# Masks, transposes and turned sums of a causal attention put into other TensorE tilings, with filler matmuls at the start

## The chip, the core and the metric

The kernel runs on one core of a Trainium2 chip. The metric is the device time of one execution in microseconds; the time of a kernel is the median of its runs. Engines are called PE (TensorE; its weight loads are PEld), DVE (VectorE), ACT (ScalarE), POOL (GpSimd) and SP (SyncE, which issues every DMA).

## The reference

```python
scores = q @ k.T / 8                      # 2 x 12 heads, 448 queries, 64 wide
scores = where(causal mask, -1e9, scores)
p = exp(scores - rowmax);  p /= (p.sum(-1) + 1e-9)
x = (p @ v) as 896 tokens x 768
h = x @ w_in                              # 768 -> 2048
g = max(h, 0) + alpha * min(h, 0)
x2 = g @ w_out                            # 2048 -> 768
g2 = sigmoid(x2 @ w_gate) * (x2 @ w_val)  # 768 -> 1536, twice
out = g2 @ w_out2                         # 1536 -> 768
```

All inputs of the attention are fp32; the weights arrive as fp64 words and are turned into fp32 on the core.

## The kernel before, in words

**Attention.** The 24 heads go in 12 pairs m. The two heads of a pair lie in partitions 0-63 and 64-127 of one tile `raw` (q and k, queries in columns). Queries and keys are cut into four chunks of 112. For each pair, `scores` (L445) computes in three groups, chunk 3, then chunks 2 and 0, then chunk 1. A score matmul has 64 rows, so that the two heads' matmuls lie in two row tiles of the array; fp32 needs two passes, each its own record. Ahead of each group `mask` (L434) writes the causal mask of the diagonal block with an identity of 112 rows in bf16, one matmul for each head.

DVE takes the negative row maxima (L464), ACT the exponentials with their sums (L475). `transposes` (L507) turns p in ten 112x112 blocks for each head into the PSUM tiles `t` (112 rows, the whole array); `copy_p` (L519) copies them to `pt` in three copies of 448, 448 and 224 columns, shared by ACT and DVE. `values` (L531) multiplies by v with 112 rows and 64 columns: the two heads lie in two column tiles. In between, `inverses` (L481) inverts the sums (112x8), `turn_sums` (L487) transposes them on PE, `copy_sums` (L492) copies them out, `spill` (L496) and `spread` (L500) take them through DRAM and spread each over 64 partitions (`rb`), and `scale_x` (L542) multiplies the result in `pv` by `rb`. POOL splits it into two fp32r parts, `xh` (L553) and `xl` (L558).

So PE works in three tilings: the whole array (masks, transposes, turned sums and all products of the feed-forward layers), two row tiles (scores), two column tiles (values).

**Feed-forward layers.** Every product is three fp32r matmuls of 128x128 by 448 columns (L631 to L633). A block of weights is loaded as words (`load_w`, L575), and turned into fp32 and split by ACT and DVE (`w_abs` L585, `w_clamp` L590, `w_shift` L595, `w_sign` L600, `w_low` L607, `w_hi` L620, `w_lo` L624). For the first four blocks `w_clamp` and `w_lo` run on POOL. The first three blocks (`NFILL`, 36 products, 108 matmuls) are "fill": they may run between the heads; those of the first six pairs' tokens need pair 5 split, those of the others pair 11.

**Order.** A planner (`Plan`, L88) writes the instruction order of all engines ahead of time: a list schedule over tasks with costs in ns, ring buffers (`take`, `use`), and a rank `base + OFFSET` that decides among tasks which could start at the same time. A task that changes PE's tiling (`mode`) is charged 185 ns. Tasks marked `late` follow only when all others are placed. PSUM has eight banks: `s0`, `s1`, `t`, `pv`, two of each. Every engine then executes in program order and waits on semaphores.

**Start.** 16 bf16 matmuls of 224 columns (L755) run ahead of the first scores. SP's first loads are, in order, q and k of pair 0, alpha, v of pair 0, weights 0, pair 1, weights 1, pair 2, weights 2.

Of the kernel before, what the change touches and what calls it, by code (L numbers as in the profile page):

```python
# [38 lines left out]
V_ORDER = (0, 3, 1, 2)
# [6 lines left out]
    ("load",): -58.635, ("load_v",): 7.783, ("scale_q",): -14.461, ("mask", 0): -68.882, ("scores", 0): -13.369,  # L46
    ("mask", 1): 11.629, ("scores", 1): -41.229, ("mask", 2): -10.666, ("scores", 2): 3.508, ("maxima", 3): -33.522,
    ("expo", 3): 77.499, ("maxima", 2): -23.050, ("expo", 2): -6.102, ("maxima", 0): -19.609, ("expo", 0): -68.639,
    ("maxima", 1): -5.168, ("expo", 1): -39.932, ("transposes", 0): -3.281, ("copy_p", 0): 49.609,
    ("transposes", 1): 2.477, ("copy_p", 1): -39.851, ("transposes", 2): -56.207, ("copy_p", 2): -58.597,  # L50
    ("values", 0): 6.339, ("values", 3): -46.358, ("values", 1): -75.999, ("values", 2): 7.714,
    ("inverses",): -60.677, ("turn_sums",): -8.582, ("copy_sums",): -11.583, ("spill",): 40.514, ("spread",): 71.632,
    ("scale_x",): -0.940, ("split_x",): -51.504, ("split_x_lo",): -23.205, None: -17.857, ("load_w", 0): 9.850,
    ("w_abs", 0): 50.945, ("w_clamp", 0): -37.063, ("w_shift", 0): -29.708, ("w_sign", 0): -30.857,
    ("w_low", 0): 6.510, ("w_hi", 0): -4.303, ("w_lo", 0): -3.032, ("h", 0, 0): 12.860, ("neg", 0, 0): 47.449,
    ("pos", 0, 0): 68.908, ("add", 0, 0): -83.306, ("g_hi", 0, 0): -8.976, ("g_lo", 0, 0): -51.651,
    ("h", 0, 1): -18.475, ("neg", 0, 1): 36.331, ("pos", 0, 1): -59.901, ("add", 0, 1): 74.082,
    ("g_hi", 0, 1): 12.898, ("g_lo", 0, 1): 6.457, ("load_w", 1): -155.678, ("w_abs", 1): 57.861,
    ("w_clamp", 1): -6.859, ("w_shift", 1): -0.546, ("w_sign", 1): -19.022, ("w_low", 1): 9.102, ("w_hi", 1): 34.782,
    ("w_lo", 1): -69.814, ("h", 1, 0): 47.300, ("neg", 1, 0): 2.091, ("pos", 1, 0): -4.691, ("add", 1, 0): 21.461,  # L60
    ("g_hi", 1, 0): -1.670, ("g_lo", 1, 0): -70.870, ("h", 1, 1): -3.830, ("neg", 1, 1): 18.865,
    ("pos", 1, 1): 41.081, ("add", 1, 1): 13.413, ("g_hi", 1, 1): 36.660, ("g_lo", 1, 1): -40.749,
    ("load_w", 2): 36.339, ("w_abs", 2): 34.065, ("w_clamp", 2): 23.745, ("w_shift", 2): -21.161,
    ("w_sign", 2): 50.694, ("w_low", 2): -5.847, ("w_hi", 2): 9.976, ("w_lo", 2): -1.386, ("h", 2, 0): 14.568,
    ("neg", 2, 0): -9.107, ("pos", 2, 0): -20.582, ("add", 2, 0): -33.620, ("g_hi", 2, 0): -17.520,
    ("g_lo", 2, 0): 14.456, ("h", 2, 1): 9.902, ("neg", 2, 1): -46.202, ("pos", 2, 1): -31.404, ("add", 2, 1): 10.874,
    ("g_hi", 2, 1): 31.747, ("g_lo", 2, 1): -27.065, ("load_w", 3): 60.447, ("w_abs", 3): -53.251,
    ("w_clamp", 3): 35.979, ("w_shift", 3): 38.519, ("w_sign", 3): 32.977, ("w_low", 3): 77.377, ("w_hi", 3): 19.462,
    ("w_lo", 3): 18.150, ("h", 0): 71.016, ("neg", 3, 0): 16.871, ("pos", 3, 0): -32.543, ("add", 3, 0): 12.093,
    ("g_hi", 3, 0): -14.119, ("g_lo", 3, 0): -32.279, ("h", 1): -17.143, ("neg", 3, 1): 41.284, ("pos", 3, 1): 18.422,  # L70
    ("add", 3, 1): 51.125, ("g_hi", 3, 1): -24.366, ("g_lo", 3, 1): -86.090, ("load_w", 4): -49.447,
    ("w_abs", 4): -41.351, ("w_clamp", 4): -15.783, ("w_shift", 4): -29.687, ("w_sign", 4): 118.991,
    ("w_low", 4): 11.679, ("w_hi", 4): 17.390, ("w_lo", 4): 38.692, ("neg", 4, 0): 85.112, ("pos", 4, 0): -25.443,
    ("add", 4, 0): -45.606, ("g_hi", 4, 0): -14.713, ("g_lo", 4, 0): -47.536, ("neg", 4, 1): 37.830,
    ("pos", 4, 1): 15.130, ("add", 4, 1): 30.215, ("g_hi", 4, 1): -15.974, ("g_lo", 4, 1): -49.843,
    ("load_w",): -88.953, ("w_abs",): -3.509, ("w_clamp",): 4.975, ("w_shift",): -96.432, ("w_sign",): -24.743,
    ("w_low",): -7.496, ("w_hi",): -67.367, ("w_lo",): -5.902, ("neg", 0): 48.678, ("pos", 0): 53.455,
    ("add", 0): 10.368, ("g_hi", 0): 34.777, ("g_lo", 0): -14.195, ("neg", 1): 27.459, ("pos", 1): -2.426,
    ("add", 1): -10.674, ("g_hi", 1): 3.570, ("g_lo", 1): 40.438, "mode": 14.580,
# [125 lines left out]
def plan_of(do):  # L205

    plan = Plan({
        "raw": 3, "vraw": 3, "s0": 2, "s1": 2, "t": 2, "pv": 2, "nm": 4, "p": 4, "sm": 2, "rs": 2, "rt": 2, "rd": 2, "rb": 2,
# [4 lines left out]
    n_heads = B * H  # L213


    for m in range(n_heads // 2):
# [13 lines left out]
        for n, chunks in enumerate(S_GROUPS):  # L230
            size = sum(c + 1 for c in chunks) * CP
            turn = [("scores", m, n - 1)] if n else prior("scores", len(S_GROUPS) - 1)
            pair("mask", "PE", 100, n, after=turn, take=[(f"s{j}", ("s", i0 + j, n)) for j in range(2)])
            pair("scores", "PE", size * PAIRED + 30, n, after=[("scale_q", m), ("mask", m, n)],
                 use=[raw, ("s", i0, n), ("s", i0 + 1, n)], mode=2)
        for i in (i0, i0 + 1):
# [16 lines left out]
            for g, kcs in enumerate(PT_GROUPS):  # L253
                n = sum(NCH - kc for kc in kcs)
                turn = [("transposes", i, g - 1)] if g else chain("transposes", len(PT_GROUPS) - 1)
                head("transposes", "PE", 96 * n, g, after=[("expo", i, c) for c in range(min(kcs), NCH)] + turn,
                     take=[("t", ("t", i, g))], use=[("p", i)])
                turn = [("copy_p", i, 0)] if g else chain("copy_p", 0)
# [4 lines left out]
        for n, kc in enumerate(V_ORDER):
            g = next(g for g, kcs in enumerate(PT_GROUPS) if kc in kcs)
            turn = [("values", m, V_ORDER[n - 1])] if n else prior("values", V_ORDER[-1]) + [("load_v", m)]
            pair("values", "PE", (NCH - kc) * CP * PAIRED + 10, kc, mode=3, after=[("copy_p", i, g) for i in (i0, i0 + 1)] + turn,
                 take=[("pv", ("pv", m))] * (n == 0),
                 use=[("pt", i0), ("pt", i0 + 1), vraw] + [("pv", m)] * (n > 0))
# [99 lines left out]
def attention_then_two_ffns(ctx: ExitStack, tc: tile.TileContext, qk, v, w_in, alpha, w_out, w_gv, w_out2, out):  # L368
# [431 lines left out]
```

## Time and profile before

| what | value |
|---|---|
| median of three runs | 610.43 us (609.7 to 612.03) |
| the profiled execution's own time | 612.99 us, span 611.2 us |
| PE busy | 597.8 us, 98% of the span, 3172 matmuls |
| DVE busy | 402.6 us, 66% |
| ACT busy | 271.4 us, 44% |
| POOL busy | 48.8 us, 8% |

A profile's page gives busy times by engine, the span in 40 slices, and the costliest groups of instructions. The same trace answers by stretches (windows), by engine in order of time (timeline: start, length, line, output<-input; "x8" means eight merged records), by tile, and as a chain of waits followed back from the last instruction. The attention takes the first 118 us, the fill that is left ends at 132.8 us, and all that follows is feed-forward.

### The profile page before, as it was taken

How to read it: one execution, taken by the hardware profiler on the slowest of the kernel's cores; microseconds unless marked ns; L12 is line 12 of the kernel's file. 1: busy time of each engine (PE TensorE's matmuls, PEld its weight loads, DVE VectorE, ACT ScalarE, POOL GpSimd, SP SyncE). 2: the span in 40 equal slices, each digit the busy share in tenths (PEclk: the TensorE clock that was granted, in tenths of full speed). 3: DMA queues.
4: the chain of work that ended last, by engine and by line, in shares of the span. 5: the costliest groups of instructions: out<-in, count | busy, mean ns of one | idle time of the engine just before them, and what ended most of it. 6: DMA issues, size and time to landing. Idle time of an engine off the chain costs nothing.

```text
span 611.2 us, 8138 instructions
## 1 busy us (share of the span) xinstructions
PE 597.8 (98%) x3172; PEld 519.9 (85%) x3172; DVE 402.6 (66%) x639; ACT 271.4 (44%) x551; POOL 48.8 (8%) x51
## 2 busy tenths in 40 slices
PE   7889999999999999999999999999999999999997
PEld 4545556799999998999999999999999999999996
DVE  2788885348888886766556766676677776655530
ACT  4777876454666553333233333333333333333320
POOL 1575422200000000000000000000000000000000
PEclk9999999999999999999999999999999999999999
DMA  8453431504333322433333333333333333344110
GB/s 273 156 163 121 122 92 32 176 11 140 104 118 105 87 94 95 137 97 129 95 108 142 104 107 107 122 116 118 103 105 105 103 104 103 109 140 149 71 45 31
DMA packets 17367, 67.82 MB, mean 111 GB/s; under 512 B 2416, under 2 KB 5488, under 8 KB 17328
## 3 DMA queue, kind: packets, MB, share of 16 engines
q1 hardware_dynamic: 17328, 67.30, 34.7%
q8 instruction: 25, 0.41, 0.3%
q14 instruction: 14, 0.11, 0.1%
HBM read 64.50 MB, written 2.80 MB: 110 GB/s over the span
## 4 chain that ended last, share of the span: by engine, by line
PE 89%; ACT 4%; DVE 4%; DMA 1%; POOL 0%; issue 0%; SPq 0%; DVEq 0%; ACTq 0%
PE s L632 26%; PE s L633 26%; PE s L631 26%; PE s L454 3%; ACT p L475 3%; PE t L514 2%; PE pv L536 2%; DVE nm L464 2%; PE s L440 1%; DMA rb<-rd 1%; PE t L633 1%; PE t L631 1%; PE t L632 1%; DVE sm L483 1%; PE s L755 1%; DVE wt L607 0%
## 5 line engine op out<-in xcount | busy, mean ns | idle before, releaser
L624 DVE TENSOR_TENSOR wl<-wt,wh 128x768 fp32r<-128x768 f32 (+1 forms) x66 | 61.6, 934 | 86.1 <-ACT wh L620 86.1
L620 ACT CAST wh<-wt 128x768 fp32r<-128x768 f32 (+1 forms) x67 | 54.7, 817 | 128.3 <-PE s L633 122.2
L632 PE MATMUL s<-x2h,wl 128*128 128x448 f32 x288 | 105.2, 365 | 0.0
L631 PE MATMUL s<-x2h,wh 128*128 128x448 f32 x288 | 105.2, 365 | 0.0
L633 PE MATMUL s<-x2l,wh 128*128 128x448 f32 x288 | 105.2, 365 | 0.0
L632 PE MATMUL s<-gp,wl 128*128 128x448 f32 x251 | 91.8, 366 | 0.3 <-DVE wl L624 0.3
L633 PE MATMUL s<-gp,wh 128*128 128x448 f32 x251 | 91.7, 365 | 0.0
L631 PE MATMUL s<-gp,wh 128*128 128x448 f32 x251 | 91.7, 365 | 0.0
L585 ACT ACTIVATE wt<-wr 128x768 f32<-128x768 f32 (+1 forms) x70 | 61.7, 884 | 31.0 <-DVE wl L624 28.6
L600 DVE SCALAR_TENSOR_TENSOR wt<-wr,wt 128x768 uint32<-128x768 uint32 (+1 forms) x70 | 65.7, 938 | 2.2
L607 DVE SCALAR_TENSOR_TENSOR wt<-wr,wt 128x768 uint32<-128x768 uint32 (+1 forms) x70 | 65.4, 934 | 2.3
L590 DVE TENSOR_SCALAR wt<-wt 128x768 f32<-128x768 f32 (+1 forms) x66 | 36.1, 547 | 33.5 <-ACT wt L585 33.5
L632 PEld LDWEIGHTS s<-x2h,wl 128*128 128x128 f32 x288 | 54.1, 188 | 4.3
L631 PEld LDWEIGHTS s<-x2h,wh 128*128 128x128 f32 x288 | 54.1, 188 | 4.3
L633 PEld LDWEIGHTS s<-x2l,wh 128*128 128x128 f32 x288 | 54.1, 188 | 4.3
L633 PE MATMUL s<-xl,wh 128*128 128x448 f32 x156 | 57.0, 365 | 0.0
L631 PE MATMUL s<-xh,wh 128*128 128x448 f32 x156 | 57.0, 365 | 0.0
L632 PE MATMUL s<-xh,wl 128*128 128x448 f32 x156 | 57.0, 365 | 0.0
L475 ACT ACTIVATE p<-s,nm 112x112 f32<-112x112 f32 (+3 forms) x96 | 46.8, 498 | 19.7 <-DVE nm L464 18.4
L632 PEld LDWEIGHTS s<-gp,wl 128*128 128x128 f32 x251 | 47.1, 188 | 4.3 <-DVE wl L624 0.6
L631 PEld LDWEIGHTS s<-gp,wh 128*128 128x128 f32 x251 | 47.1, 188 | 3.7
L633 PEld LDWEIGHTS s<-gp,wh 128*128 128x128 f32 x251 | 47.1, 188 | 3.7
(84 smaller groups left out, 840.6 us busy)
## 6 DMA issues: line engine op xcount, KB each, us to landing
wr<-in_w_gv SPq DMA_DIRECT2D x24, 768.0 KB, 4.5
wr<-in_w_out SPq DMA_DIRECT2D x18, 768.0 KB, 4.2
wr<-in_w_in SPq DMA_DIRECT2D x16, 768.0 KB, 4.4
wr<-in_w_out SPq DMA_DIRECT2D x12, 640.0 KB, 4.1
raw<-in_qk SPq DMA_DIRECT2D x12, 448.0 KB
vraw<-in_v SPq DMA_DIRECT2D x12, 224.0 KB, 2.5
rb<-rd SPq DMA_DIRECT2D x24, 112.0 KB, 4.0
out_t<-a SPq DMA_DIRECT2D x12, 224.0 KB, 1.9
```

Of the source, the lines that this page charges most:

```text
L454: nc.tensor.matmul(s[:, o:o + w], lhsT=q[:, c * CP:w], rhs=k[:, :w], start=False, stop=c == chunks[-1], skip_group_check=True,)
L464: nc.vector.tensor_reduce(out=tiles["nm", i][:, c:c + 1], in_=tiles["sc", i, c], axis=AX.X, op=ALU.max, negate=True)
L475: nc.scalar.activation(out=tiles["p", i][:, P_OFF[c]:P_OFF[c] + (c + 1) * CP], in_=tiles["sc", i, c], func=AF.Exp, bias=tiles["nm", i][:, ...
L585: nc.scalar.activation(out=t.bitcast(F32), in_=tiles["wr", n][:, :, 1].bitcast(F32), func=AF.Abs)
L590: engine("w_clamp", n).tensor_scalar(f, f, F64_LO, F64_HI, ALU.max, ALU.min)
L600: nc.vector.scalar_tensor_tensor(out=t, in0=tiles["wr", n][:, :, 1], scalar=0xC0000000, in1=t, op0=ALU.bitwise_and, op1=ALU.bitwise_or)
L607: nc.vector.scalar_tensor_tensor(out=t, in0=tiles["wr", n][:, :, 0], scalar=29, in1=t, op0=ALU.logical_shift_right, op1=ALU.bitwise_or)
L620: nc.scalar.copy(out=new_w("wh", n, ring), in_=tiles["wt", n].bitcast(F32))
L624: engine("w_lo", n).tensor_tensor(out=new_w("wl", n, ring), in0=tiles["wt", n].bitcast(F32), in1=tiles["wh", n].bitcast(F32), op=ALU.subtract)
L631: nc.tensor.matmul(ps, lhsT=wh_, rhs=a, start=(k == 0), stop=False)
L632: nc.tensor.matmul(ps, lhsT=wl_, rhs=a, start=False, stop=False)
L633: nc.tensor.matmul(ps, lhsT=wh_, rhs=c, start=False, stop=(k == last))
```

## The change

- `mask` is done by halves of 56 queries: a 56x128 selector (`ones_b`) in rows 0-55 for one head and rows 64-119 for the other, 112 columns for the first half and 56 for the second; the two heads' matmuls lie in the two row tiles of the scores.
- A transposed block is two transposes: of 64 queries in rows 0-63 into `t`, and of 48 queries in rows 64-111 into a new bank `u`. The copies are now 8 x 64, 2 x 64 and 10 x 48 columns for each head.
- `turn_sums` is a plain fp32 matmul with 64 columns of weights (`rsums`, zero beyond 8), in the values' column tiling.
- `values` is one task for the pair and needs all three copies of both heads. `pv` has one bank, `u` one.
- The warm-up matmuls are 40 tasks of two (56 rows, 224 columns), of the lowest rank, placed by the planner where PE would pause, and all ahead of the first values, whose bank they hold.
- `load_w` 0 comes after q and k of pair 4; `w_clamp` is always on DVE. Ranks and the engines of `copy_p` are others.

```diff
-PT_GROUPS = ((0,), (1, 3), (2,))
+PT_BLOCKS = [(kc, c) for kc in (0, 1, 3, 2) for c in range(kc, NCH)]
+LOW, HIGH, HALF = 64, CP - 64, CP // 2
-N_WARM = 16
+N_WARM = 40
...
-COPY_P = ("ACT", "DVE", "ACT"), ("ACT", "ACT", "DVE")
+COPY_P = ("ACT", "ACT", "DVE"), ("ACT", "DVE", "ACT")
...
-        "raw": 3, "vraw": 3, "s0": 2, "s1": 2, "t": 2, "pv": 2, "nm": 4, "p": 4, "sm": 2, "rs": 2, "rt": 2, "rd": 2, "rb": 2,
+        "raw": 3, "vraw": 3, "s0": 2, "s1": 2, "t": 2, "u": 1, "pv": 1, "nm": 4, "p": 4, "sm": 2, "rs": 2, "rt": 2, "rd": 2, "rb": 2,
...
+    add(("warm", -1), "PE", 1700, lambda rings: None)
+    for n in range(N_WARM):
+        add(("warm", n), "PE", 330 if n < 7 else 190, do("warm", n), base=100, after=[("warm", n - 1)], mode=2,
+            take=[("pv", "warm")] * (n == 0), use=["warm"] * (n > 0), step=("warm",))
...
-            pair("mask", "PE", 100, n, after=turn, take=[(f"s{j}", ("s", i0 + j, n)) for j in range(2)])
+            pair("mask", "PE", 110, n, mode=2, after=turn, take=[(f"s{j}", ("s", i0 + j, n)) for j in range(2)])
...
-        pair("turn_sums", "PE", 100, after=[("inverses", m)], use=[("rs", m)], take=[("t", ("tr", m))])
+        pair("turn_sums", "PE", 200, mode=3, after=[("inverses", m)], use=[("rs", m)], take=[("t", ("tr", m))])
...
-        step("load_w", "SP", 450, after=chain("load_w"), lag=100, dma=2900 * wide, take=[("wr", wr)])
+        step("load_w", "SP", 450, after=chain("load_w") if n else [("load", 4)], lag=100, dma=2900 * wide, take=[("wr", wr)])
-        step("w_clamp", "POOL" if early else "DVE", 820 if early else 150 + 405 * wide, after=[("w_abs", n)], use=[wt], port=True)
+        step("w_clamp", "DVE", 150 + 405 * wide, after=[("w_abs", n)], use=[wt], port=True)
...
+        for half in range(2):
+            for j in range(2):
+                rows = slice(j * D, j * D + HALF)
+                s = tiles["s", 2 * m + j, n][:, at:at + wide * CP].rearrange("p (c k) -> p c k", k=CP)
+                nc.tensor.matmul(
+                    s[:, :, half * HALF:], lhsT=ones_b[rows, half, :], rhs=mask_b[rows, :wide, :CP - half * HALF],
+                    start=(half == 0), stop=False, skip_group_check=True,
+                )
...
-        nc.tensor.transpose(t[:2 * NCH, :CP], tiles["rs", m].rearrange("p j c -> p (j c)"), ident[:CP, :CP])
+        nc.tensor.matmul(t[:D, :CP], lhsT=rsums[m % 2], rhs=ident[:CP, :CP], start=True, stop=True)
...
+            nc.tensor.transpose(low[:CP, n * LOW:(n + 1) * LOW], p[:LOW, block], ident[:LOW, :LOW])
+            o = (8 * g + n) * HIGH
+            nc.tensor.transpose(tiles["u", i][:CP, o:o + HIGH], p[LOW:CP, block], ident[LOW:CP, LOW:CP])
...
-        nc.scalar.activation(out=mask_b[:, :CP], in_=ident[:CP, :CP], func=AF.Exp)
+        nc.scalar.activation(out=mask_f, in_=ident[:, :CP], func=AF.Exp)
```

## Rows read from the trace of the kernel before

**Rows 1.** Busy us by stretch: PE, PEld, DVE, ACT, POOL; granted clock, DMA.
```profile
core 0: us, PE busy (x) PEld busy (x) DVE busy (x) ACT busy (x) POOL busy (x), PEclk, DMA share, GB/s
5.75:18.85 13.10, 11.65 (x46) 6.19 (x46) 5.28 (x13) 6.53 (x22) 3.90 (x3) 1.00 0.80 256
18.85:118.10 99.25, 93.84 (x703) 57.81 (x701) 74.04 (x174) 74.59 (x235) 41.73 (x38) 1.00 0.38 113
118.10:132.80 14.70, 14.70 (x72) 13.56 (x73) 5.08 (x8) 4.75 (x10) 2.02 (x2) 1.00 0.31 126
132.80:607.90 475.10, 474.67 (x2341) 439.21 (x2339) 317.18 (x439) 183.52 (x284) 0.00 (x0) 1.00 0.33 105
...
20.00:60.00 40.00, 36.67 (x277) 21.28 (x277) 34.56 (x80) 33.11 (x104) 24.25 (x19) 1.00 0.53 162
```

**Rows 2.** PE's waits over the whole span: the last of six.
```profile
PE s L632 <- DVE wl L624: 0.3, 1, 0.3
```

**Rows 3.** PE's timeline over one pair: start, length, line, output<-input, records.
```profile
53.01 0.31 PE L440 MATMUL s<-mask_b,ident_b 112*112 112x112 bf16 x2
53.16 0.94 PE L514 MATMUL t<-ident,p 112*112 112x112 f32 x8
54.02 0.64 PE L454 MATMUL s<-raw 64*112 64x224 f32 x4
54.59 0.31 PE L440 MATMUL s<-mask_b,ident_b 112*112 112x112 bf16 x2
54.74 0.36 PE L514 MATMUL t<-ident,p 112*112 112x112 f32 x2
55.03 1.01 PE L454 MATMUL s<-raw 64*112 64x448 f32 x4
55.97 0.98 PE L514 MATMUL t<-ident,p 112*112 112x112 f32 x8
56.78 0.35 PE L440 MATMUL s<-mask_b,ident_b 112*112 112x224 bf16 x2
57.07 1.02 PE L454 MATMUL s<-raw 64*112 64x336 f32 x8
58.01 0.40 PE L514 MATMUL t<-ident,p 112*112 112x112 f32 x2
```

**Rows 4.** The chain of waits: eight of those transposes.
```profile
53.32 0.77 PE t L514 x8
```

**Rows 5.** PE's timeline at the start: warm-up, and first scores of pair 1.
```profile
2.81 3.15 PE L755 MATMUL s<-mask_b,ident_b 112*112 112x224 bf16 x16 [2.81 <-DVE mask_b L751]
...
15.23 1.84 PE L454 MATMUL s<-raw 64*112 64x448 f32 x4
```

**Rows 6.** POOL's timeline: scaling of pair 1's q, and one clamp of weights.
```profile
10.22 0.57 POOL L431 TENSOR_SCALAR raw<-raw 128x448 f32<-128x448 f32 x1 [8.44 <-DMA raw<-in_qk]
...
39.56 2.77 POOL L590 TENSOR_SCALAR wt<-wt 128x768 f32<-128x768 f32 x1
```

**Rows 7.** DVE's timeline: sums of pairs 1 and 9 ready, one clamp.
```profile
24.08 0.17 DVE L483 TENSOR_SCALAR sm<-sm 112x8 f32<-112x8 f32 x1
...
63.59 0.63 DVE L590 TENSOR_SCALAR wt<-wt 128x768 f32<-128x768 f32 x1 [0.33 <-ACT wt L585]
...
89.25 0.17 DVE L483 TENSOR_SCALAR sm<-sm 112x8 f32<-112x8 f32 x1 [0.74 <-ACT p L475]
```

**Rows 8.** ACT's copies of 448 columns out of PSUM, 0 to 118 us.
```profile
L528 ACT COPY pt<-t 112x448 f32<-112x448 f32 x36 | 18.4, 538 | 5.8 <-PE t L514 5.7
```

**Rows 9.** Pair 5's sums on their way: DVE, SP, landings of `rb`, `scale_x`.
```profile
61.07 0.25 DVE L493 COPY rt<-t 8x112 f32<-8x112 f32 x1
...
61.35 0.28 SPq L497 DMA_DIRECT2D rd<-rt  x1
...
63.16 1.09 SPq L504 DMA_DIRECT2D rb<-rd  x2
...
DMA to landing us min/median/max: 2.9/4.0/6.8
...
L543 DVE TENSOR_TENSOR xf<-pv,rb x12: 602/609/626, 36.8 to 118.2; 128x448 f32<-128x448 f32 x12
```

More of the change, by code (lines that the diff above doesn't have):

```diff
@@ L34 @@
 S_GROUPS = ((3,), (2, 0), (1,))
-PT_GROUPS = ((0,), (1, 3), (2,))
+PT_BLOCKS = [(kc, c) for kc in (0, 1, 3, 2) for c in range(kc, NCH)]
+LOW, HIGH, HALF = 64, CP - 64, CP // 2
 NPT = 10 * CP
 BANK = 512
-N_WARM = 16
-V_ORDER = (0, 3, 1, 2)
+N_WARM = 40
 F64_LO, F64_HI = 2.0 ** -15, 122879.9921875
 OFFSET = {
[L46 to L79, printed above, removed]
@@ new lines @@
+    None: -41.144, ("warm",): 13.275, ("load",): -63.306, ("load_v",): 12.704, ("scale_q",): -21.133,
+    ("mask", 0): -3.898, ("scores", 0): -4.327, ("mask", 1): -26.049, ("scores", 1): -51.058, ("mask", 2): -3.748,
+    ("scores", 2): -23.184, ("maxima", 3): -46.264, ("expo", 3): 60.604, ("maxima", 2): -1.560, ("expo", 2): 6.022,
+    ("maxima", 0): 1.695, ("expo", 0): -40.951, ("maxima", 1): -1.503, ("expo", 1): -37.167,
+    ("transposes", 0): -1.799, ("transposes", 1): -21.727, ("copy_p", 0): -22.971, ("copy_p", 1): -72.141,
@@ new lines @@
+    ("copy_p", 2): -62.693, ("values",): 2.188, ("inverses",): 10.458, ("turn_sums",): -8.060, ("copy_sums",): 3.372,
+    ("spill",): -1.341, ("spread",): 64.643, ("scale_x",): -16.464, ("split_x",): 11.023, ("split_x_lo",): -53.682,
+    ("load_w", 0): 33.586, ("w_abs", 0): -41.827, ("w_clamp", 0): -33.373, ("w_shift", 0): 9.489,
+    ("w_sign", 0): -46.627, ("w_low", 0): 32.596, ("w_hi", 0): -41.452, ("w_lo", 0): -19.938, ("h", 0, 0): 14.886,
+    ("neg", 0, 0): 52.825, ("pos", 0, 0): 13.008, ("add", 0, 0): -58.456, ("g_hi", 0, 0): -52.984,
@@ L252, in plan_of @@
                          use=[("s", i, n), ("nm", i)] + [("p", i)] * (not lead) + [("sm", m)] * (not lead or i > i0))
[L253 to L258, printed above, removed]
-                eng = COPY_P[i % 2][g]
-                head("copy_p", eng, 75 + 0.82 * n * CP if eng == "ACT" else 100 + 1.045 * n * CP, g,
-                     after=[("transposes", i, g)] + turn,
-                     use=[("t", i, g)] + [("pt", i)] * (g > 0), take=[("pt", ("pt", i))] * (g == 0))
@@ L263, in plan_of @@
[L263 to L268, printed above, removed]
+            for g, n in enumerate((8, 2)):
+                turn = [("transposes", i, 0)] if g else chain("transposes", 1)
+                head("transposes", "PE", 96 * n, g, mode=2, after=[("expo", i, c) for c in range(NCH)] + turn,
+                     take=[("t", ("t", i, g))] + [("u", ("u", i))] * (g == 0), use=[("p", i)] + [("u", i)] * g)
@@ new lines, in plan_of @@
+            for g, n in enumerate((8 * LOW, 2 * LOW, 10 * HIGH)):
+                eng = COPY_P[i % 2][g]
+                head("copy_p", eng, 75 + 0.82 * n if eng == "ACT" else 100 + 1.045 * n, g,
+                     after=[("transposes", i, min(g, 1))] + ([("copy_p", i, 0)] if g else chain("copy_p", 0)),
+                     use=[("u", i) if g == 2 else ("t", i, g)] + [("pt", i)] * (g > 0), take=[("pt", ("pt", i))] * (g == 0))
+        pair("values", "PE", sum(range(NCH + 1)) * CP * PAIRED + 40, mode=3, take=[("pv", ("pv", m))],
+             after=[("copy_p", i, g) for i in (i0, i0 + 1) for g in range(3)] + prior("values") + [("load_v", m)],
+             use=[("pt", i0), ("pt", i0 + 1), vraw])
@@ L274, in plan_of @@
         pair("spread", "SP", 580, after=[("spill", m)], use=[("rd", m)], take=[("rb", ("rb", m))], lag=100, dma=1100)
-        pair("scale_x", "DVE", 620, after=[("values", m, V_ORDER[-1]), ("spread", m)], use=[("pv", m), ("rb", m)],
+        pair("scale_x", "DVE", 620, after=[("values", m), ("spread", m)], use=[("pv", m), ("rb", m)],
              take=[("xf", ("xf", m))])
@@ L404, in attention_then_two_ffns @@
     ident = const.tile([P, P], F32, name="ident")
-    ident_b = const.tile([CP, CP], BF16, name="ident_b")
-    mask_f = const.tile([CP, CP], F32, name="mask_f")
-    mask_b = const.tile([CP, 2 * CP], BF16, name="mask_b")
+    ones_b = const.tile([P, 2, P], BF16, name="ones_b")
+    mask_f = const.tile([P, CP], F32, name="mask_f")
+    mask_b = const.tile([P, 2, CP], BF16, name="mask_b")
+    rsums = [const.tile([CP, D], F32, name=f"rsums{n}") for n in range(2)]
     alpha_sb = const.tile([P, NF], F32, name="alpha_sb")
@@ L417, in engine, with warm @@
         return engines[plan.tasks[name]["eng"]]
+    @task
+    def warm(n, ring=None):
+        if ring is not None:
+            new("warm", ring, [P, S], F32)
+        for i in range(2):
+            nc.tensor.matmul(
+                tiles["warm"][:, :2 * CP], lhsT=ones_b[:HALF, 0, :], rhs=mask_b[:HALF].rearrange("p c k -> p (c k)"),
+                start=(n + i == 0), stop=(n == N_WARM - 1 and i == 1),
+            )
     @task
@@ L446, in scores @@
         chunks = S_GROUPS[n]
-        banks = [tiles["s", 2 * m + j, n] for j in range(2)]
+        banks = [tiles["s", 2 * m + j, n][:CP] for j in range(2)]
         o = 0
@@ L506, in transposes @@
     @task
-    def transposes(i, g, ring):
-        p, kcs = tiles["p", i], PT_GROUPS[g]
-        t = new(("t", i, g), ring, [CP, S], F32)
-        base = PT_OFF[kcs[0]]
-        for kc in kcs:
-            for c in range(kc, NCH):
-                o = PT_OFF[kc] - base + (c - kc) * CP
-                nc.tensor.transpose(
-                    t[:, o:o + CP], p[:, P_OFF[c] + kc * CP:P_OFF[c] + (kc + 1) * CP], ident[:CP, :CP]
-                )
+    def transposes(i, g, *rings):
+        p = tiles["p", i]
+        low = new(("t", i, g), rings[0], [P, S + LOW], F32)
+        if g == 0:
+            new(("u", i), rings[1], [P, S + LOW], F32)
+        for n, (kc, c) in enumerate(PT_BLOCKS[:8] if g == 0 else PT_BLOCKS[8:]):
+            block = slice(P_OFF[c] + kc * CP, P_OFF[c] + (kc + 1) * CP)
+            nc.tensor.transpose(low[:CP, n * LOW:(n + 1) * LOW], p[:LOW, block], ident[:LOW, :LOW])
+            o = (8 * g + n) * HIGH
+            nc.tensor.transpose(tiles["u", i][:CP, o:o + HIGH], p[LOW:CP, block], ident[LOW:CP, LOW:CP])
     @task
@@ L530, in values @@
     @task
-    def values(m, kc, ring=None):
-        if ring is not None:
-            new(("pv", m), ring, [P, S], F32)
-        o, n = PT_OFF[kc], (NCH - kc) * CP
-        for j in range(2):
-            nc.tensor.matmul(
-                tiles["pv", m][j * D:(j + 1) * D, kc * CP:], lhsT=tiles["v", m][:, kc, j, :],
-                rhs=tiles["pt", 2 * m + j][:, o:o + n], start=ring is not None, stop=kc == V_ORDER[-1],
-            )
+    def values(m, ring):
+        t = new(("pv", m), ring, [P, S], F32)
+        for kc in range(NCH):
+            o, n = PT_OFF[kc], (NCH - kc) * CP
+            for j in range(2):
+                nc.tensor.matmul(
+                    t[j * D:(j + 1) * D, kc * CP:], lhsT=tiles["v", m][:, kc, j, :],
+                    rhs=tiles["pt", 2 * m + j][:, o:o + n], start=(kc == 0), stop=(kc == NCH - 1),
+                )
     @task
@@ L742, in attention_then_two_ffns @@
         make_identity(nc, ident)
-        nc.scalar.activation(out=mask_b[:, :CP], in_=ident[:CP, :CP], func=AF.Exp)
-        nc.vector.tensor_copy(out=ident_b, in_=ident[:CP, :CP])
+        nc.scalar.activation(out=mask_f, in_=ident[:, :CP], func=AF.Exp)
+        nc.vector.memset(ones_b, 0.0)
         nc.gpsimd.memset(mask_f, 0.0)
-        nc.gpsimd.affine_select(
-            out=mask_f, in_=mask_f, pattern=[[-1, CP]], compare_op=ALU.is_ge, fill=-8e9, base=0, channel_multiplier=1
-        )
+        for j in range(2):
+            rows = slice(j * D, j * D + HALF)
+            for half in range(2):
+                nc.vector.tensor_copy(
+                    out=ones_b[rows, half, half * HALF:(half + 1) * HALF], in_=ident[rows, j * D:j * D + HALF]
+                )
+            nc.gpsimd.affine_select(
+                out=mask_f[rows], in_=mask_f[rows], pattern=[[-1, CP]], compare_op=ALU.is_ge, fill=-8e9, base=0,
+                channel_multiplier=1,
+            )
         for c in range(2):
-            nc.vector.tensor_copy(out=mask_b[:, c * CP:(c + 1) * CP], in_=mask_f)
-        t = psum.tile([P, S], F32, tag="s0", name="s0", bufs=size["s0"])
-        for n in range(N_WARM):
-            nc.tensor.matmul(t[:CP, :2 * CP], lhsT=ident_b, rhs=mask_b, start=(n == 0), stop=(n == N_WARM - 1))
+            nc.vector.tensor_copy(out=mask_b[:, c, :], in_=mask_f)
+        for t in rsums:
+            nc.vector.memset(t, 0.0)
         for _, name, rings in plan.order():
```

53 lines of the change are left out of this document (40 added, 13 removed).

## The prediction

> **What bounds the kernel now.** I read the busy times by stretch first. From 132.8 us on PE is busy 474.67 of 475.10 us [rows 1], and over the whole span it waits once for weights there, 0.3 us [rows 2]. The change leaves every matmul of that part as it is, so its 475 us stay, and time can only come from the 132.8 us before. There PE is busy 93.84 of 99.25 us during the attention, while DVE is busy 74.04 and ACT 74.59, three quarters [rows 1]: PE sets the pace, the other two follow at a distance. The 14.70 us after it are 72 of the 108 fill matmuls, 0.204 us each, back to back; 54 of these need pair 11, so this block cannot shrink much, and what the attention gains is what the kernel gains.
>
> A busy PE is not a useful PE. The timeline of one pair, 53.01 to 58.01 us, shows it [rows 3]. A transpose of 112 columns takes 0.77/8 = 0.096 us [rows 4]; I take that for one fp32 pass of 112 columns anywhere. The 5.00 us hold 18 transposes before the one at 58.01, 20 passes of scores (2 x (2+4+3+1), two heads side by side) and masks of 8 x 112 bf16 columns at half the price: 38 x 0.096 + 8 x 0.048 = 4.03 us. The other 0.97 us fall on six changes between full-array work and scores, 0.16 us each: eight transposes from 53.16 should end at 53.93, the scores start at 54.02, and their 4 passes' worth takes 0.57 instead of 0.38 us.
>
> **The change part by part.**
>
> *Tilings.* Masks, transposes and scores now share one tiling, turned sums and values another. Of a pair's eight changes the six above go: 12 x 0.97 = -11.6 us of PE. Against it, fill products stood among transposes of their own tiling and now stand alone: 36 matmuls, 12 products, were placed inside the attention (108 less 72). In one piece that is 2 changes, in twelve 24 x 0.16 = 3.9 us; I take +2.
>
> *Transposes.* 240 blocks cost 240 x 0.096 = 23.0 us. The halves stream 64 and 48 columns. No row shows transposes side by side. If they run like the two heads' scores, a block costs 64/112 x 0.096 = 0.055 us: -9.8 us. One after the other, 0.055 + 0.041: 0. Each half still loads 112 columns of weights; if that sets the pace and the loads queue, 2 x 0.096: +23. The nearest row is the scores at 55.03: four records of 448 columns, which alone would take 4 x 0.384 = 1.54 us, are over in 0.94 [rows 3], so tiles do run side by side, loads too. I take 0.060: -8.6 us.
>
> The Trainium skill, TensorEngine Tiling (Array Packing), section Performance Considerations, speaks against this: every matmul carries about 60 cycles beside its columns, so one should not tile a dimension that is already small. At 2.4 GHz that would be, as an estimate, 25 ns on each: 0.080 us a block and -3.8 us instead of -8.6. The trace shows no such share: 112-column masks, two in the 0.15 us from 54.59 to 54.74 [rows 3], leave little room for it even with a refill of the array.
>
> *Masks and turned sums.* A mask chunk was 2 x 0.048 and is 168 columns side by side, 0.072; over a pair 0.38 becomes 0.29: -1.2 us in all. The turned sums need two passes instead of one: 12 x 0.096 = +1.2. They cancel.
>
> *Start.* The first scores of pair 1 take 1.84 us, the same form at 55.03 takes 1.01 [rows 5, 3]: until about 18.85 us PE runs at half its rate, the 1.2 GHz level, although the granted clock column says 1.00 there. Its 11.65 us of work [rows 1] would be 5.8 us at the full level: the bound of what fillers can save; the other is 0, if they don't lift the clock. Pair 1's q is there only at 10.22 us, since weights were loaded ahead of it [rows 6], and its scores wait until 15.23; without the weights it comes earlier. I take -4 for both. The 80 fillers cost 0.19 us each at the low level (3.15/16) [rows 5], 0.09 to 0.19: 7 to 15 us, hidden only in real pauses; the planner puts about seven pairs, 2.6 us, where now 16 stand, and they begin later because POOL's clearing of the mask now follows ACT's write. For both +0.5, between 0 and 4.
>
> PE in all: -11.6 + 2 - 8.6 - 4 + 0.5 = -21.7 us.
>
> *DVE and ACT.* Four clamps of 0.63 us come to DVE [rows 7]: +2.5 us; POOL is rid of 2.77 us each [rows 6], which DVE's next step had to wait for. The copies carry the same 1120 columns a head in three pieces; ACT gets 64 columns more for each pair, 64/448 x 0.538 x 12 = +0.9 us at most [rows 8]. So DVE must do 74.04 + 2.5 = 76.5 us in what was 99.25. In its fullest 40 us it was busy 34.56, 86%, ACT 33.11, 83% [rows 1]. At 88% the stretch needs 87 us: -12 us. This, and not PE's -18 (without the start), is what the middle can give.
>
> *Waits.* The one bank `u` makes a head's transposes wait for the copy of the head before, up to 0.54 us [rows 8] x 23 = 12 us; I take 0, because the scores of another pair (2 us) lie between. Values wait for all copies of both heads: nothing, if scores stand ahead of them. SP: `load_w` 0 waits behind the load of pair 4, and the spill and spread of pair 0 behind it; the weights aren't needed until pair 5 is split, tens of us later. After the attention DVE has 5.08 of 14.70 us to do [rows 1], so weights that came late are caught up there.
>
> **Sum.** Start -3.5 net, middle -12, and +1 for pieces of wait that move (bounds 0 and +4): -14.5. The profiled execution took 612.99 us (span 611.2); that gives 598.5. The median of the runs shown, 610.43, lies 2.56 below it: **596 us**, 590 to 601 for this case.
>
> **Rivals.**
>
> 1. *DVE and ACT get no fuller than 80%.* For: both wait for each other inside a head (maxima, exponentials, copies), and their mean is 75%. Against: 86% in the 40 us with weights. 76.5/0.80 = 96 us: -3.6, with the start -7: 604 us (601 to 607). At 75% the stretch is 102 us, which eats the start: 610, no change. The Trainium skill says this in TensorEngine Tiling (Array Packing), section PSUM Bottleneck: tiling speeds up PE, not the copies out of PSUM. The rows above bear it out so far.
>
> 2. *One bank `pv` sets the pace: slower.* With the turned sums in the values' tiling, the order pays if they stand right before the values, and then `pv` is held until the sums are back. From rows: copy to spill 0.28, spill to spread 1.81, spread to landing 4.0 in the median and 6.8 at most, `scale_x` 0.61 [rows 9], with the turn itself about 0.5: 7.2 us for each pair in the median, 10.0 at most. Sums become ready every (89.25 - 24.08)/8 = 8.15 us now [rows 7]. Below a landing of about 4.9 us it costs nothing against before; with 5.9 in the mean, 9.1 us a pair, it costs 11 x 1.0 = 11 us, less 4 of the start: 617 us. For: weights now land in the middle of the attention. Against: the sums can be turned one pair ahead.
>
> 3. *PE's whole -21.7 shows*, because fill products close its pauses and DVE's waits shrink with POOL's clamps gone: 589 us.
>
> 4. *It doesn't do what it says*: loads of the two tiles queue, or fillers stand where PE had work. Half blocks at 0.13 us (+8) take most of what the tilings give: 610 us.
>
> **How the numbers follow.** Forecast 0.58; rival 1 at 604 0.20; rival 2 0.07; rival 3 0.06; no change by 75% or by rival 4 0.09. Two runs of this kernel can be told apart from about 0.5%, 3 us. Faster than 607.4: 0.58 + 0.20 + 0.06 = 0.84; same 0.09; slower than 613.5 0.07. The range of 8 in 10 is 586 to 607: it leaves out rival 2, no change, and a little below.
>
> **What would show it.** In PE's timeline masks, transposes and scores should follow each other without the 0.1 us before and the 0.1 us inside each group; ten blocks of a head in 0.6 us (right), 1.0 (serial) or 1.9 (loads). Scores of pair 1 should begin before 13 us at 1.01 us. The stretch of the attention should end near 104 us, with DVE at 85% or more; a pair every 7.1 us. It is wrong if PE waits for `xf` ahead of the values (rival 2), if the attention ends after 112 us with DVE below 80% (rival 1), or if the stretch from the first late product on is no longer 475 us.

## The result and the profile after

The changed kernel takes 606.73 us, the median of ten runs (600.5 to 612.94), against 611.23 (609.7 to 614.31) for ten runs of the kernel before on the same chip: ratio 0.9894 [0.9851, 0.9938]. (Ratios are of the means, here 605.16 and 611.62 us, and leave out the one run that counts as slow, 612.94 us.) The forecast was 596: the kernel is faster, clear of the spread of the runs but by less than 2%, and by 4.5 us instead of 14.5. The profiled execution took 608.03 us, with a span of 606.2 us. The page gives the busy times:

```profile
PE 593.8 (98%) x3560; PEld 520.8 (86%) x3560; DVE 401.9 (66%) x649; ACT 266.9 (44%) x551; POOL 36.4 (6%) x48
```

The stretches that answer to [rows 1], for the changed kernel: the start, the attention in two parts, the fill after it, and the rest.

```profile
5.88:16.00 10.12, 9.98 (x108) 8.26 (x105) 6.04 (x17) 5.93 (x22) 1.69 (x3) 1.00 0.51 143
16.00:56.00 40.00, 38.05 (x482) 25.93 (x480) 30.98 (x79) 32.67 (x113) 12.15 (x14) 0.96 0.63 190
56.00:105.90 49.90, 46.83 (x557) 31.99 (x553) 41.19 (x97) 39.19 (x124) 19.09 (x20) 1.00 0.35 105
105.90:120.50 14.60, 14.60 (x74) 13.55 (x73) 5.09 (x8) 4.96 (x10) 2.03 (x2) 1.00 0.37 150
120.50:602.40 481.90, 481.64 (x2340) 439.07 (x2340) 316.93 (x439) 181.71 (x283) 0.00 (x0) 1.00 0.32 103
```

The attention ends at 105.9 instead of 118.1 us, the first late product starts at 120.5 instead of 132.8: 12.3 us are gained there. The rest, the same matmuls, takes 481.9 instead of 475.1 us by these windows; from the first late product's start to the last one's start it is 481.9 after 474.6, so 7.3 us are lost again. 612.99 - 12.3 + 7.3 = 608.0: that is the whole difference between the two profiled executions.

The lost part begins at one place. PE's timeline of the changed kernel (start, length, line) at the only late wait, which answers to [rows 2]:

```profile
222.66 0.36 PE L656 MATMUL s<-gp,wh 128*128 128x448 f32 x1
223.28 0.47 PE L657 MATMUL s<-gp,wl 128*128 128x448 f32 x1 [0.26 <-DVE wl L649]
223.60 0.36 PE L658 MATMUL s<-gp,wh 128*128 128x448 f32 x1
223.80 0.37 PE L656 MATMUL s<-gp,wh 128*128 128x448 f32 x1
```

Before the wait, matmuls start every 0.2027 us in the mean; after it every 0.2067 us, to the end. 1834 matmuls x 0.0040 = 7.3 us. The granted clock is 1.00 on both sides, and no wait and no idle time shows: PE is "busy" throughout. Only the count in a window tells it (the x behind PE):

```profile
230.00:330.00 100.00, 100.00 (x485) 90.85 (x484) 62.39 (x88) 29.16 (x41) 0.00 (x0) 1.00 0.37 117
```

What the change was to do to PE's groups, it did. PE's timeline of one pair (compare [rows 3]):

```profile
27.38 0.25 PE L459 MATMUL s<-mask_b,ones_b 56*128 56x112 bf16 x4
27.47 0.98 PE L474 MATMUL s<-raw 64*112 64x448 f32 x4
28.29 0.31 PE L459 MATMUL s<-mask_b,ones_b 56*128 56x224 bf16 x4
28.44 0.97 PE L474 MATMUL s<-raw 64*112 64x336 f32 x8
29.25 0.22 PE L535 MATMUL t<-ident,p 64*112 64x64 f32 x1
29.25 0.26 PE L537 MATMUL u<-ident,p 48*112 48x48 f32 x2
...
29.75 0.22 PE L535 MATMUL t<-ident,p 64*112 64x64 f32 x1
```

Masks, scores and transposes follow each other with no gap. The four records of 448 columns, whose successor started 0.94 us later before, are over in 28.29 - 27.47 = 0.82 us. A transposed block takes 0.055 us (ten starts of the 64-row half, 0.055 apart in the mean, from 29.25 to 29.75), below the 0.060 that was taken. Counted over the trace, PE changes its tiling 38 times instead of 93.

### The profile page after: what moved, and what is told of

Read it like the earlier page. It is cut to its first block, busy times and chain, and to the rows that moved or that the text cites. A ratio compares the mean times of both kernels' runs of the same rounds, so it can differ in the third digit from the quotient of the medians.

```text
span 606.2 us, 8918 instructions
## 1 busy us (share of the span) xinstructions
PE 593.8 (98%) x3560; PEld 520.8 (86%) x3560; DVE 401.9 (66%) x649; ACT 266.9 (44%) x551; POOL 36.4 (6%) x48
## 4 chain that ended last, share of the span: by engine, by line
PE 88%; ACT 5%; DVE 4%; DMA 1%; issue 1%; POOL 0%; SPq 0%; DVEq 0%; POOLq 0%; ACTq 0%
PE s L657 27%; PE s L656 27%; PE s L658 27%; ACT p L495 3%; PE s L474 2%; DVE nm L484 1%; PE pv L561 1%; ACT pt L553 1%; PE pv L429 1%; DMA rd<-rt 1%; DVE wt L632 1%; DMA rb<-rd 0%; PE s L459 0%; DVE xf L568 0%; ACT wh L645 0%
## 5 line engine op out<-in xcount | busy, mean ns | idle before, releaser
L657 PE MATMUL s<-gp,wl 128*128 128x448 f32 x264 | 97.2, 368 | 0.3 <-DVE wl L649 0.3
L656 PE MATMUL s<-gp,wh 128*128 128x448 f32 x264 | 97.1, 368 | 0.0
L658 PE MATMUL s<-gp,wh 128*128 128x448 f32 x264 | 97.1, 368 | 0.0
L615 DVE TENSOR_SCALAR wt<-wt 128x768 f32<-128x768 f32 (+1 forms) x70 | 38.9, 555 | 31.8 <-ACT wt L610 31.3
L495 ACT ACTIVATE p<-s,nm 112x336 f32<-112x336 f32 (+3 forms) x96 | 47.3, 519 | 19.2 <-DVE nm L484 19.2
L657 PEld LDWEIGHTS s<-gp,wl 128*128 128x128 f32 x264 | 49.6, 188 | 5.6 <-DVE wl L649 0.6
L658 PEld LDWEIGHTS s<-gp,wh 128*128 128x128 f32 x264 | 49.5, 188 | 5.0
L656 PEld LDWEIGHTS s<-gp,wh 128*128 128x128 f32 x264 | 49.6, 188 | 5.0
```

The source lines that it names most:

```text
L495: nc.scalar.activation(out=tiles["p", i][:, P_OFF[c]:P_OFF[c] + (c + 1) * CP], in_=tiles["sc", i, c], func=AF.Exp, bias=tiles["nm", i][:, ...
L615: nc.vector.tensor_scalar(f, f, F64_LO, F64_HI, ALU.max, ALU.min)
L656: nc.tensor.matmul(ps, lhsT=wh_, rhs=a, start=(k == 0), stop=False)
L657: nc.tensor.matmul(ps, lhsT=wl_, rhs=a, start=False, stop=False)
L658: nc.tensor.matmul(ps, lhsT=wh_, rhs=c, start=False, stop=(k == last))
```

## The experiments

The question was where 10 of the 14.5 us are. All runs below count from the kernel before on the same chip, whose medians in these jobs were 612.33, 613.97 and 612.10 us.

**The changed kernel again.** 

> The changed kernel once more, nothing edited. Theory A (two paces): PE's matmuls of the feed-forward layers run at one of two paces, 0.2027 or 0.2067 us each, and the pause of 0.6 us near 223 us decides which one follows; so single runs fall into two groups, about 599 to 601 us (pace kept) and 605 to 609 us (1834 matmuls x 0.004 = 7.3 us more), and the trace taken shows one of the two paces from the first matmul after the pause to the end. Theory B (the changed kernel's tiles or the chip's power slow PE after some 220 us, whatever PE did): every run has 0.2067 us from about there on, and the spread of the runs has another cause.

Six runs, median 603.28 us (600.6 to 607.71), ratio 0.9859 [0.9816, 0.9903]. The profiled one took 600.6 us, with the same wait (0.26 us, the next matmul at 223.15), and the pace stays at 0.2027 us. The same windows as above, of this execution:

```profile
120.40:594.90 474.50, 474.24 (x2340) 439.14 (x2339) 316.60 (x439) 181.59 (x283) 0.00 (x0) 1.00 0.32 105
230.00:330.00 100.00, 100.00 (x495) 92.67 (x494) 63.35 (x90) 29.82 (x42) 0.00 (x0) 1.00 0.39 124
```

495 matmuls instead of 485 in the same 100 us, from one and the same program. So the instructions do not fix the pace. By their spans (some 7 us longer, where the rest is alike), 7 of the kernel's 16 runs were at the 0.2067 us pace, and of 40 runs of the kernel before in the later jobs 2 (617.03 and 617.04 us).

**No wait at the turn.** The wait stands where the products turn from one matrix to the next. The first products of the second then have to come behind the last of the first, so that a weight buffer becomes free earlier.

```
 ... after=[("w_lo", n), needs(...)] + before
+ + [("h", NF - 1, c, KD - 1) for c in range(B)] * (n == NF and k == 0),
```

> The changed kernel with one more order rule: the first products of the second layer wait, in the planned order, for the last products of the first, so that no weight buffer is held across the turn and PE has no pause there. Theory A: with no pause PE keeps the pace with which it began, 0.2027 us over all 2340 late matmuls, all runs lie near 599 us less the 0.7 us of the pause itself: 598 to 601, against 611 for the kernel before and a median near 606 for the changed one. Theory B: 0.2067 us from about 220 us on as in the changed kernel, 606 us. If the pace is drawn anew by other things too, single runs still fall into two groups.

Six runs, median 600.68 us (599.72 to 605.28), ratio 0.9834 [0.9797, 0.9871]. PE has no wait left in the feed-forward layers, 2412 matmuls run in one go, and the stretch is as long as before:

```profile
120.10:594.00 473.90, 473.90 (x2340) 439.26 (x2339) 316.78 (x439) 181.63 (x282) 0.00 (x0) 1.00 0.32 105
```

**The same kernel once more.** 

> The version without the pause once more, nothing edited, for more single runs. By theory A none of them is in the slow pace (none of 19 runs of versions without the pause was, 7 of 16 of the changed kernel were): 598 to 600 us where PE's clock rises near 10 us, some 4 us more where it rises near 18 us, as in the trace of the changed kernel with the small matmuls of zeros. If the pace is drawn at the start of the feed-forward stretch as well, about a third of the runs lie near 609 us (2411 x 0.004 = 9.6 us more).

Median 600.8 us (599.57 to 605.5), ratio 0.9841 [0.9803, 0.9880]. By their spans none of the 12 runs was at the slower pace, against 7 of 16 with the wait (on the one chip that ran both, none of 6 against 2 of 6), and all eight traces of kernels without the wait keep 0.2027 us to the end. In its median this version lies below both kernels; against the changed one the ratios of single jobs overlap (0.9834 [0.9797, 0.9871] and 0.9859 [0.9816, 0.9903]), and it is the count of runs that tells them apart. In the profiled execution PE's rate rose from its lower to its higher level only at 21.43 us, called "late" below, and not near 10 us ("early"); the part on the prediction takes that up.

**The same rule in the kernel before.** 

> The kernel before with the same order rule, so that PE has no pause between the two layers. If the rule is worth only the pause, 0.7 us, here too, since the kernel before is rarely in the slow pace (2 of 33 runs at 617 us), the median falls by 0 to 1 us to about 611 to 612; if what the rule does in the changed kernel comes from something else than the pace, it falls by 3 us or more. Against it the version without the pause shows what the change is worth with the pace out of play: the traces with a like rise of the clock give 8 to 9 us.

12 runs, median 611.61 us, ratio 0.9995 [0.9974, 1.0016]: nothing to be seen. The kernel before waits 0.3 us as well [rows 2], and its wait was seldom followed by the slower pace. Why the changed kernel falls into it so much oftener stays open.

**Twelve small matmuls in the row.** A small matmul of zeros, of 64 rows (another tiling) or 128 rows by turns, goes into every fourth block of weights from the 20th on; it adds zero to the sums. It was put into both kernels, with the wait left in, and each ran once (608.54 us, and 614.72 for the kernel before).

```
+KICKS = {20 + 4 * n: ((D, P)[n % 2], 16 + 16 * (n // 2)) for n in range(12)}
...
+        if n in KICKS and n not in kicked and k == k0 + 2:
+            ...
+            nc.tensor.matmul(ps[:rows, :w], lhsT=zero_b[:rows, :rows], rhs=zero_b[:rows, :w], start=False, stop=False, ...)
```

> The changed kernel with twelve small matmuls of zeros added into sums of the feed-forward layers, one in every fourth weight block from the 20th on; every other one has 64 rows (PE must change its tiling, a short stop), the others 128 rows (no change), with 16 to 96 columns; results stay the same. Theory A: the pace between two of them is either 0.2027 or 0.2067 us throughout, and changes, if it does, only at one of them, rather at those that stop PE. Theory B: 0.2067 us everywhere from 220 us on. Time: 12 x about 0.3 us more than the changed kernel, plus or minus what the paces make.

> The kernel before with the same twelve small matmuls of zeros. Theory A: the two paces belong to the chip and not to the change, so that some of the thirteen stretches run at 0.2067 us here too, although the profiled execution of the kernel before held 0.2027 throughout. Theory B: 0.2027 us in all stretches, since the kernel before has neither the new tiles nor the new order.

Between these matmuls the pace is one of two values, 202.67 or 206.67 ns, constant over a stretch, and it changes only at one of them. In the changed kernel 2 of the 13 stretches are at 206.67, from 249.6 and from 355.6 us on; in the kernel before 4 of 13, from 254.7, 333.6, 390.5 and 449.9 us on. First the small matmul at 249 us and three windows of 22 us, each within one stretch, of the changed kernel; x108 is the slower pace, x110 or x111 the faster:

```profile
248.88 0.37 PE L670 MATMUL s<-gp,wh 128*128 128x448 f32 x1
249.17 0.19 PE L663 MATMUL s<-zero_b 64*64 64x16 bf16 x1
249.30 0.47 PE L668 MATMUL s<-gp,wh 128*128 128x448 f32 x1
```

```profile
251.00:273.00 22.00, 22.00 (x108) 19.97 (x108) 13.07 (x19) 5.75 (x8) 0.00 (x0) 1.00 0.31 96
277.00:299.00 22.00, 22.00 (x110) 20.39 (x109) 13.80 (x20) 6.41 (x10) 0.00 (x0) 1.00 0.31 97
...
357.00:379.00 22.00, 22.00 (x108) 19.97 (x108) 13.68 (x19) 8.12 (x12) 0.00 (x0) 1.00 0.31 108
```

The same for the kernel before, with the small matmul at 333 us:

```profile
256.00:278.00 22.00, 22.00 (x108) 19.99 (x107) 13.13 (x19) 5.70 (x8) 0.00 (x0) 1.00 0.31 96
282.00:304.00 22.00, 22.00 (x111) 20.39 (x110) 13.81 (x20) 6.33 (x10) 0.00 (x0) 1.00 0.31 96
...
335.00:357.00 22.00, 22.00 (x108) 19.97 (x108) 14.82 (x19) 8.42 (x11) 0.00 (x0) 1.00 0.31 108
363.00:385.00 22.00, 22.00 (x110) 20.39 (x109) 13.96 (x20) 8.12 (x12) 0.00 (x0) 1.00 0.32 108
```

```profile
333.04 0.37 PE L645 MATMUL s<-gp,wh 128*128 128x448 f32 x1
333.25 0.19 PE L638 MATMUL s<-zero_b 128*128 128x32 bf16 x1
333.29 0.45 PE L643 MATMUL s<-gp,wh 128*128 128x448 f32 x1
```

In the changed kernel both slower stretches begin at a matmul of 64 rows, which PE starts 0.30 us after the one ahead of it. In the kernel before one of the four does; the other three begin at one of 128 rows, which starts 0.21 us after the one ahead, at PE's usual pace: no stop is needed. Every slower stretch ended at the next small matmul. So the pace is drawn anew where the row of equal matmuls is broken, in both kernels, and does not belong to the change. Weights, DMA and the other engines look alike on both sides.

**Few fillers.** Without the wait, and with 14 of the 80 fillers.

```
+        if n >= 7:
+            return
...
```

> The version without the pause, with the first 7 filler tasks (14 matmuls) alone; the other 66 matmuls are left out, all else stands in the same order. Theory C (the fillers lift the clock): PE's matmuls run at half rate until about 15 to 19 us instead of 10, the sums of pair 1 are ready 2 to 4 us later than at 20.3 us, and the attention ends at 108 to 110 us instead of 105.6. Rival D (the fillers stand in PE's way, or do nothing): it ends at 105.6 or up to 1 us earlier. The runs would lie at 602 to 604 by C, 599 by D.

Four runs, median 601.25 us (600.21 to 602.62), ratio 0.9808 [0.9756, 0.9859]; the attention ends at 105.90 us, against 105.60 in the version without the wait. PE was at its higher level by 12.83 us here too:

```profile
12.83 1.01 PE L477 MATMUL s<-raw 64*112 64x448 f32 x4
```

So the other 66 fillers were not needed for it, and bring at most 0.3 us. They may do one other thing, which 4 runs don't show: the mean granted clock is below 0.998 in 3 of these 4 runs, in 2 of 12 with all fillers, and in 30 of 40 runs of the kernel before.

**What bounds the attention?** Four kernels, all without the wait, each changing mainly the load of one engine in it: no clamp of the first five blocks (DVE does less), no absolute value of them (ACT does less; the clamp then reads the loaded words), the old masks on the whole array, the old transposes on the whole array with copies of 448, 224 and 448 columns (PE does more, with more changes of tiling).

```
 def w_clamp: +  if n < NFILL + 2: return
 def w_abs:   +  if n < NFILL + 2: return
 def mask:    +  one matmul a head, lhsT=ident_b (112 rows), rhs=mask_w, for every pair but 0
 def transposes:
-            nc.tensor.transpose(low[:CP, n * LOW:(n + 1) * LOW], p[:LOW, block], ident[:LOW, :LOW])
-            nc.tensor.transpose(tiles["u", i][:CP, o:o + HIGH], p[LOW:CP, block], ident[LOW:CP, LOW:CP])
+            nc.tensor.transpose(to[:CP, o:o + CP], p[:, block], ident[:CP, :CP])
```

> The version without the pause, with the clamp of the first five weight blocks left out (0.56 us each on DVE, 2.8 us in all, during the attention; weights outside the clamp's bounds would come out wrong). Theory E (DVE sets the pace in the middle of the attention, where it is 90% busy from 36 to 86 us): the attention ends 2 to 3 us earlier than at 105.6 us. Rival F (PE sets the pace, as in the kernel before): within 0.5 us of 105.6.

> The version without the pause, with the absolute value of the first five weight blocks left out (0.92 us each on ACT, 4.6 us in all; the clamp reads the loaded words instead, so negative weights of these blocks come out wrong). Theory H (ACT sets the pace of the attention): it ends 3 to 4.5 us earlier than at 105.6 us. Theory G (no engine's sum sets it: maxima, exponentials, transposes and copies wait for each other along a fixed order): within 1 us, as with 2.8 us less on DVE.

> The version without the pause, with the masks of pairs 1 to 11 again as one matmul of 112 rows for each head over the whole array, in the same order: 33 groups, each with two changes of tiling that the changed kernel does not have. At 0.16 us a change that is 66 x 0.16 = 10.6 us of PE, and 1.1 us for the masks themselves. Theory F (PE sets the pace everywhere): the attention ends 10 to 12 us later than at 105.6. Theory E (DVE and ACT set it in the middle): half of it or less, 3 to 6 us.

> The version without the pause, with the transposes again as whole 112x112 blocks over the whole array, 4, 4 and 2 blocks to the three banks, in the same order and with copies of 448, 224 and 448 columns. A block should take 0.096 us instead of 0.055 (240 x 0.041 = 9.8 us of PE), and each of the 48 groups mostly two changes of tiling (up to 96 x 0.16 = 15 us, less where groups touch values). Theory F: the attention ends 17 to 25 us later than at 105.6, later than in the kernel before. Theory E: 8 to 15 us later, since DVE and ACT leave PE slack in the middle.

The windows from zero to the end of the attention: the version without the wait, then the one without the clamps too (both early; its runs took 599.67 and 599.74 us):

```profile
0.00:105.60 105.60, 96.38 (x1149) 67.52 (x1149) 79.26 (x202) 79.26 (x258) 34.47 (x46) 1.00 0.47 146
```

```profile
0.00:105.40 105.40, 96.25 (x1149) 67.38 (x1149) 76.99 (x197) 79.27 (x258) 33.62 (x46) 1.00 0.50 145
```

2.3 us less of DVE's time (busy, third number of the engines) moves the end by 0.2: DVE's sum is no bound. The same for ACT, where both executions were late, with the rise at 21.4 us, the version without the wait first (the one without the absolute values ran in 603.62 and 598.90 us):

```profile
0.00:110.80 110.80, 101.42 (x1149) 71.52 (x1149) 79.53 (x202) 79.71 (x258) 34.43 (x46) 1.00 0.48 139
```

```profile
0.00:109.40 109.40, 100.74 (x1149) 71.27 (x1150) 79.58 (x202) 76.07 (x253) 34.83 (x46) 1.00 0.48 140
```

3.6 us less of ACT move the end by 1.4, more than the 1 us of the one theory and less than the 3 of the other. The old masks raise the changes of tiling from 38 to 96 and end the attention at 107.97, 2.4 us later (runs of 602.25 and 605.01 us). Their group, from the first mask to the transposes, takes 53.91 - 51.46 = 2.45 us, against 52.13 - 50.25 = 1.88 without them; the first timeline is with them:

```profile
51.46 0.41 PE L461 MATMUL s<-mask_w,ident_b 112*112 112x112 bf16 x2
...
53.91 0.22 PE L546 MATMUL t<-ident,p 64*112 64x64 f32 x1
```

```profile
50.25 0.23 PE L460 MATMUL s<-mask_b,ones_b 56*128 56x112 bf16 x3 [0.29 <-ACT p L496]
...
52.13 0.22 PE L536 MATMUL t<-ident,p 64*112 64x64 f32 x1
```

0.57 us for these two groups of each pair would be 6.3 us for 11 pairs, and 2.4 of it arrive: PE's sum is no bound either. The old transposes (77 changes) end the attention at 114.57 us, late, against 109.9 for the changed kernel with the small matmuls, which come after the attention, and as late (both rise near 18.8 us): 4.7 us; seven runs, median 606.49 us (604.84 to 608.91), ratio 0.9883 [0.9847, 0.9920]. So every part of PE's work counts for something, none in full, and none of the three engines sets the pace by its sum. The chain of waits in the version without the wait agrees (36 to 86 us; start, length, engine, tile):

```profile
38.74 0.50 DVE nm L485
40.53 2.12 ACT p L496 x10
...
60.74 0.48 PE s L475 x4
61.22 2.04 PE pv L562 x16
63.51 0.68 DVE nm L485 x2
...
70.30 3.03 DMA rd<-rt
...
73.85 2.79 DMA rb<-rd
...
77.05 0.62 DVE xf L569
```

It goes from maxima to exponentials, copies, products and the next maxima, over all three engines by turns, while each has 45.37 (PE), 45.11 (DVE) and 42.57 (ACT) busy us of these 50. Once, at 70.30 us, it leads through DRAM with the sums of one pair, though DVE is busy until their `scale_x` and names no wait for `rb`. That the fixed order of this chain is the bound is argued from here, not shown by a run, and what the trip through DRAM costs was not tried.

## Why the prediction was wrong

**The step that failed** is "The change leaves every matmul of that part as it is, so its 475 us stay". The matmuls are as they were, but their time is not settled by them alone: with the wait at the turn the changed kernel took 481.9 us for them in one execution and 474.5 in another. That is +7.3 us, half of the forecast's gain, in 7 of 16 runs; with the wait taken away the stretch was 473.9 us. The term stood at nothing in the sum, and what decides which pace follows stays open. [Rows 1] could not show it: the 2341 matmuls in 475.10 us are 0.2029 each, one of two paces. The last line of the part on what would show it named this stretch as the place to look.

**"Start -3.5 net"** came out in the profiled execution (sums of pair 1 at 19.77 instead of 24.08 us, [rows 7]), but by luck: little of it was the change. PE reached its higher level at 8.85 us there, at about 10 in the second profile, and at 21.43 in one of the same program but for the order rule; at 18.85 in the profile of before, and at 8.15 in the one of before with the small matmuls. With the rise about alike the sums of pair 1 come at 19.77 (rise at 8.85) or 20.31 us (rise near 10) instead of 20.83 (rise at 8.15), and at 24.09 instead of 24.08 (both late):

```profile
20.83 0.17 DVE L486 TENSOR_SCALAR sm<-sm 112x8 f32<-112x8 f32 x1
```

```profile
20.31 0.17 DVE L503 TENSOR_SCALAR sm<-sm 112x8 f32<-112x8 f32 x1 [1.76 <-ACT p L495]
```

```profile
24.09 0.17 DVE L506 TENSOR_SCALAR sm<-sm 112x8 f32<-112x8 f32 x1 [1.61 <-ACT p L498]
```

These are the kernel before with the small matmuls, the changed kernel again, and the changed one with the small matmuls: the start is worth 0 to 1.1 us. The two levels show in the same twelve fillers of the version without the wait, in two executions of one program:

```profile
9.61 1.48 PE L430 MATMUL pv<-mask_b,ones_b 56*128 56x224 bf16 x12
```

```profile
9.61 2.44 PE L430 MATMUL pv<-mask_b,ones_b 56*128 56x224 bf16 x12
```

A late rise costs some 5 us: attention end 105.60 against 110.77, spans 598.1 against 603.2.

**"Middle -12" and +1 for pieces of wait** is -8.2 to -8.7: from the sums of pair 1 to the end of the attention 94.0 us became 85.3 (early) and 85.8 (late); like for like the end itself goes from 114.9 to 105.6 and from 118.1 to 109.9. So this term too is some 2 to 3 us short. The term was worked out from DVE at 88%; it is 80% (72.06 of 89.60 us, 16 to 105.6). That is the share of rival 1, but not its reason alone: taking 2.3 us from DVE moves the end by 0.2. The forecast treated DVE's share as a bound; these runs speak for a result, of a chain that was not tried by itself.

**PE's terms for the tilings were right**, as far as rows show them. Changes of tiling went from 93 to 38, and putting 58 of them back costs 2.4 us; transposes take 0.055 a block instead of 0.060; masks stand without a gap. The prediction read the Trainium skill, TensorEngine Tiling (Array Packing), section Performance Considerations, as 60 cycles added to each matmul, an estimate of 0.080 us a block: no such addition shows in the 0.055 us. The section also says that one column takes as long as 60; as a floor, that would leave the 64 columns as they are. The row of masks that the prediction set against it did not settle it: at its own 0.048 us for 112 columns, two masks leave 0.054 of 0.15 us, 0.027 each, as much as the 25 ns. That PE's -21.7 would not arrive in full was right too.

**The rivals.** `pv` did not set the pace: PE's waits name no `xf` ahead of the values, DVE's no `rb`. Loads of the two tiles don't queue. In the version without the wait the gain is 11.3 to 11.7 us in the median, which fits the like-for-like 8 to 9 us with the dips of the clock that the kernel before has more often: its runs have spans of 607.8 us at a mean granted clock of 1.000, 610.5 at 0.994 and 612.2 at 0.992. Against that the later rise is commoner with the change, 8 of 28 runs by their spans.

## What to carry to other kernels

Before a stretch is set down as untouched, look at its pace over time (matmuls in equal windows), not at its busy time: after a stop of 0.3 us the next 379 us had another pace. Where PE runs dense for hundreds of microseconds, a single short wait in it can be worth removing, as here in the changed kernel, though not in the one before; and of a gain near the noise, several executions have to be profiled. A share of busy time at which an engine was seen is no price for the work that is put on it; take some away on the chip first.

## What the runs showed of the hardware

- A dense row of 128x128 by 448 fp32r matmuls has two steady paces, 202.67 and 206.67 ns, at the same granted clock of 1.00; which one holds can change where the row is broken, by a wait of 0.26 us, by a small matmul in another tiling, or by one of 128 rows and 32 columns ahead of which PE did not stop, and is then kept, over up to 379 us. What decides which stays open: the same wait at nearly the same time (223.28 and 223.15 us) gave one and the other.
- The rise of PE's rate from the lower level (224-column fillers 0.19 us apart) to the higher came between 8 and 13 us in some executions and at 18 to 21 us in others, in one program too (9.94 and 21.43 us), while the granted clock column said 1.00. With 66 fillers left out it had come by 12.83 us.
